# More output buffers, a moved half of one output stage, an earlier weight quarter, and zero matmuls in waits: attention and a swish layer on one core

## The chip, the core and the metric

The kernel runs on one core of a Trainium2 chip (trn2). The core has five engines with a queue of instructions each: TensorE (PE; its weight loads are PEld), VectorE (DVE), ScalarE (ACT), GpSimd (POOL) and SyncE (SP). GpSimd, SyncE and ScalarE also issue DMAs, which 16 DMA engines carry out. The metric is the device time of one execution in microseconds (us), less is better.

## What is computed

For each of 8 batches and 8 heads: attention over 576 positions with a window of 128, a bias that falls linearly with distance, and head dimension 64. The heads of a token side by side make 512 features, and the 4608 tokens then go through two matrix products with a swish between them.

```python
scores = q @ k.T / 8 - slope[h] * abs(rel)      # only 0 <= rel < 128
attn   = softmax(scores)
x      = (attn @ v) as [4608 tokens, 512]
h      = x @ w_in                                # 512 -> 2048
g      = h * sigmoid(beta * h)
out    = g @ w_out                               # 2048 -> 512
```

## The kernel before

A batch goes through these helpers. `load_pair` (L100), `load_tail`, `load_qk` and `load_v` each start a DMA on SP into a staging buffer (`fst`, 16 of them, L78) and a cast to bf16 on GpSimd. Batches 0 to 2 are transposed on TensorE (`TP`, `TT`: transposes into PSUM, then a VectorE copy), the later ones by transposing DMAs on SP (`TD`, L223). `SC` (L235) makes a block of scores (L240, L254) in a PSUM tile of the pool `psum_s`, which has one buffer, and ScalarE takes the exponentials (L262, L267). `PV` (L283) multiplies by the values for four heads (g = 0 or 1) of one block of 128 queries, into PSUM of `psum_t` (two buffers, shared with all transposes), and normalizes: a reciprocal and a multiply on VectorE, or, for batch 0 and g = 1, four multiplies on ScalarE (L305). `X` (L312) transposes the normalized block through `psum_t` into `XT`, with a ScalarE copy for batch 0 and a VectorE copy otherwise.

The layer works in nine groups of 512 tokens. `HS(g, j)` (L330) is one of 16 slices of the hidden layer: four matmuls of 512 columns (L337) into `psum_h`, a tanh on ScalarE (L342) and a combining instruction on VectorE (L343). Groups 0 to 2 let every second slice use `psum_o` as well, so four buffers instead of two (L334). `OS(g, i, n)` (L347) is a quarter of the output of 128 tokens, four matmuls (L353) into `psum_o`; after the fourth quarter ScalarE evicts the tile to an output buffer (`osb`, three of them, L84, L359) and GpSimd issues its store (L361).

The order of TensorE is the order of the program text; that of the other engines is planned by the compiler around it. TensorE does, in this order: batch 0's transposes, scores and values (L454 to L479); the 16 slices of group 0 with batch 1 spread between them (L494); the 16 slices of group 1 alone (L499); the 32 quarters of the outputs of groups 0 and 1 with batch 2 spread between them (L502); group 2's slices with batch 3 (L507, no output among them); then for each later group its slices in turn with the quarters of the group before, and the remaining batches between them; last the 16 quarters of group 8 (L517). `spread` sets so many attention steps behind each item that they end three items before the end of the list.

W1 is loaded in four quarters and W2 too, by DMAs on GpSimd that also cast (L172, L175). The first two quarters of W1 are issued behind the cast of the fourth block of V of batch 0 (L431), the third and fourth behind casts of batch 1 (L437), W2 behind those of V of batch 1.

Of the kernel before, what the change touches and what calls it, by code (L numbers as in the profile page):

```python
# [11 lines left out]
BF16 = mybir.dt.bfloat16  # L12
F32 = mybir.dt.float32
P = 128
# [3 lines left out]
def kernel(  # L18
# [10 lines left out]
    nc = tc.nc  # L29
# [38 lines left out]
    kpos = const.tile([P, 1], F32, name="kpos")  # L68
    bias = const.tile([P, 2, H], F32, name="bias")
    VS = [const.tile([P, NQB, H, D + 2], BF16, name=f"vs{i}") for i in range(2)]  # L70
    QK = [const.tile([P, 2, NP, NQB * P], BF16, name=f"qkT{i}") for i in range(2)]
# [5 lines left out]

    fst_pool = ctx.enter_context(tc.tile_pool(name="fst", bufs=16))  # L78
    bst_pool = ctx.enter_context(tc.tile_pool(name="bst", bufs=8))
# [3 lines left out]
    sig_pool = ctx.enter_context(tc.tile_pool(name="sig", bufs=3))  # L83
    osb_pool = ctx.enter_context(tc.tile_pool(name="osb", bufs=3))  # L84
    psum_s = ctx.enter_context(tc.tile_pool(name="psum_s", bufs=1, space=bass.MemoryType.PSUM))
# [13 lines left out]

    def load_pair(b, p):  # L100
        t = bst_pool.tile([P, 2, LA, 2, D], BF16, name="bst", tag="bst")
        for i, src in enumerate((q, k)):
            f = fst_pool.tile([P, 2, LA, D], F32, name="fst", tag="fst")
            nc.sync.dma_start(
                out=f[:].rearrange("r h a d -> r h (a d)"),
                in_=src[b, 2 * p : 2 * p + 2, 0:LM].rearrange("h (r a) d -> r h (a d)", a=LA),
            )
            c = nc.gpsimd.tensor_copy(out=t[:, i], in_=f[:].rearrange("r h a d -> r a h d"))
        staged[b, p] = t
        return c  # L110
# [14 lines left out]
    def load_v(b, sb):  # L125
# [10 lines left out]
        allow_small_or_imprecise_dtypes=True,  # L136
    )
    nc.vector.tensor_scalar(out=ident[:], in0=diff[:], scalar1=0.0, scalar2=None, op0=ALU.is_equal)
    nc.vector.memset(QK[0][:, :, :, S:], 0.0)
# [50 lines left out]
    def load_beta():  # L190
        bps = psum_t.tile([P, NFF], F32, name="bps", tag="t")
        nc.tensor.transpose(out=bps[:], in_=bflat[:], identity=ident_f[:])
        return nc.vector.tensor_scalar_mul(beta_h[:], bps[:], 0.5)


# [86 lines left out]

    def PV(b, qb, g):  # L283
        nq = ROWS[qb]
        vs = VS[b % 2]
        if g == 0:
            xns[b, qb] = xn_pool.tile([P, H, D], BF16, name="xn", tag="xn")
        xn = xns[b, qb]
        pv = psum_t.tile([P, 4, 66], F32, name="pv", tag="t")
        for hl in range(4):  # L290
            h = 4 * g + hl
            if qb:
                nc.tensor.matmul(  # L293
                    pv[:, hl, 0 : D + 1], lhsT=weights(b, qb - 1, h, 1),
                    rhs=vs[:, qb - 1, h, 0 : D + 1], start=True, stop=False,
                )
            nc.tensor.matmul(  # L297
                pv[:, hl, 0 : D + 1], lhsT=weights(b, qb, h, 0),
                rhs=vs[:, qb, h, 0 : D + 1], start=qb == 0, stop=True,
            )  # L300
        zs = xn_pool.tile([P, 4, 1], F32, name="zs", tag="zs")
        rcp = nc.vector.reciprocal(out=zs[0:nq], in_=pv[0:nq, :, D : D + 1])  # L302
        if b == 0 and g:
            for hl in range(4):
                nc.scalar.mul(xn[0:nq, 4 + hl, :], pv[0:nq, hl, 0:D], zs[0:nq, hl, :])  # L305
            return rcp
        nc.vector.tensor_tensor(  # L307
            out=xn[0:nq, 4 * g : 4 * g + 4, :], in0=pv[0:nq, :, 0:D],
            in1=zs[0:nq].broadcast_to([nq, 4, D]), op=ALU.mult,
        )  # L310

    def X(b, qb):  # L312
# [17 lines left out]
    def HS(g, j):  # L330
        if j == 0:
            gts[g] = gt_pool.tile([P, NFF, TOKG], BF16, name="gT", tag="gT")
        c0 = (g * TOKG) % XTR
        pool, tag = (psum_o, "ops") if g < 3 and j % 2 else (psum_h, "hps")  # L334
        hps = pool.tile([P, TOKG], F32, name="hps", tag=tag)
# [11 lines left out]
    def OS(g, i, n):  # L347
# [9 lines left out]
        if n == 3:  # L357
            osb = osb_pool.tile([P, DM], F32, name="osb", tag="osb")
            nc.scalar.mul(osb[:], ops_[:], 0.5)  # L359
            row0 = g * TOKG + i * P  # L360
            nc.gpsimd.dma_start(out=out[row0 : row0 + P, :], in_=osb[:])  # L361

# [63 lines left out]
    with tc.manual_schedule(engines={mybir.EngineType.PE}):  # L426
# [7 lines left out]
        for p in range(NP):  # L434
            c = load_pair(1, p)
            if p % 2:
# [10 lines left out]
        with tc.tile_pool(name="psum_x", bufs=2, space=bass.MemoryType.PSUM) as psum_x:  # L447
            pools = [psum_x, psum_x, psum_s]

            def sc0(m, p):  # L450
                SC(0, m, p, pools[0])
                pools.append(pools.pop(0))

            TP(0, 0)  # L454
            TP(0, 1)
# [17 lines left out]
        psum_o = ctx.enter_context(  # L473
            tc.tile_pool(name="psum_o", bufs=2, space=bass.MemoryType.PSUM))
        for qb in range(NQB):
            c = PV(0, qb, 1)
            if qb:
                X(0, qb - 1)
        X(0, NQB - 1)  # L479
        with tc.issue_after(c.ins):  # L480
# [20 lines left out]
        ahead(2, 1)()  # L501
        spread(os(0) + os(1), by_pair(2))  # L502
        todo = sum((by_block(b) for b in range(NTE, B)), [])
# [3 lines left out]
        for g in range(2, NTG):  # L507
            moe = hs(g)
            if g > 2:
                moe = sum(([a, c] for a, c in zip(moe, os(g - 1))), [])  # L510
# [38 lines left out]
```

## Time and profile before

| | us |
|---|---|
| median of 3 runs (lowest to highest) | 367.81 (366.11 to 368.38) |
| the profiled execution | 365.09 |
| its span, first to last instruction | 363.3 |
| TensorE busy | 327.8 (90%) |
| ScalarE, VectorE, GpSimd busy | 215.7, 203.0, 102.2 |
| HBM read, written | 36.71 MB, 9.44 MB |

The profile shows one execution. A line of the busy table gives an engine's busy time in a stretch; the slices cut the span into 40 parts of 9.08 us and give tenths. The granted clock is TensorE's, as a share of its full 2.4 GHz; the lower level is 0.50. A wait is put down to the instruction or DMA that released it last. Times within the span count from its first instruction.

### The profile page before, as it was taken

Reading aid. Unit: us, or ns where it says so; the run is one execution under the profiler, and the core shown is the slowest. Engines: PE = TensorE matmul, PEld = TensorE weight load, DVE = VectorE, ACT = ScalarE, POOL = GpSimd, SP = SyncE. Lnnn points to the kernel's source line nnn. Section 1 sums busy time; section 2 is a strip of 40 time slices with the busy share of each in tenths; the row PEclk is TensorE's granted clock in tenths of the full one; section 3 lists DMA queues with packets and bytes.
Section 4 is the critical chain, followed back from the end, with each engine's and each line's share of the span. In section 5 each row is a group of like instructions: output and inputs, shape, how many; then the busy total and the mean of one; then the engine's idle time right before and its main releaser. Section 6 shows DMA issues by size and latency. Waiting matters only on the chain.

```text
span 363.3 us, 6317 instructions
## 1 busy us (share of the span) xinstructions
PE 327.8 (90%) x2317; PEld 159.9 (44%) x2361; DVE 203.0 (56%) x441; ACT 215.7 (59%) x427; POOL 102.2 (28%) x176
## 2 busy tenths in 40 slices
PE   2967998999659797899999999999999999999993
PEld 1444454454325343444444445444444445444441
DVE  5435768766325288656566756675766556433300
ACT  4575784756241588575675876686768674444410
POOL 6672552424364063126145010200000000100111
PEclk9976999999969989999999999999999999999998
DMA  7999999979999698979899513200000000010021
GB/s 193 246 251 230 229 212 229 181 154 160 188 257 242 133 251 142 174 142 209 188 211 250 105 43 81 80 28 32 31 29 31 29 31 31 37 50 32 29 87 58
DMA packets 125886, 48.26 MB, mean 133 GB/s; under 512 B 113296, under 2 KB 123552, under 8 KB 125856
## 3 DMA queue, kind: packets, MB, share of 16 engines
q1 hardware_dynamic: 118720, 34.22, 50.4%
q0 software_dynamic: 7104, 13.63, 14.1%
q8 instruction: 18, 0.29, 0.3%
q14 instruction: 12, 0.10, 0.1%
q10 hardware_dynamic: 32, 0.01, 0.0%
HBM read 36.71 MB, written 9.44 MB: 127 GB/s over the span
## 4 chain that ended last, share of the span: by engine, by line
PE 42%; issue 34%; DMA 6%; DVE 5%; ACT 4%; POOL 3%; SPq 3%; POOLq 0%; ACTq 0%
PE hps L337 18%; PE ops L353 13%; PE sps L254 3%; DMA fst<-in_v_dram 3%; POOL out_dram L361 3%; PE sps L240 2%; PE pv L297 2%; PE pv L293 2%; SPq L94 2%; SPq L226 2%; PE xt L320 1%; DVE gT L343 1%; DMA fst<-in_q_dram 1%; ACT xn L305 1%; DVE xn L307 1%
## 5 line engine op out<-in xcount | busy, mean ns | idle before, releaser
L337 PE MATMUL hps<-XT,W 128*128 128x512 bf16 x550 | 143.8, 385 | 1.7 <-issue 0.9
L353 PE MATMUL ops<-W,gT 128*128 128x512 bf16 x559 | 143.9, 383 | 1.1 <-issue 0.3
L342 ACT ACTIVATE sig<-hps,beta_h 128x512 bf16<-128x512 f32 x144 | 99.5, 692 | 72.8 <-PE hps L337 63.4
L343 DVE SCALAR_TENSOR_TENSOR gT<-sig,hps 128x512 bf16<-128x512 bf16 x144 | 98.4, 684 | 56.3 <-ACT sig L342 55.7
L267 ACT ACTIVATE pt<-sps,bias 128x256 bf16<-128x256 f32 (+1 forms) x192 | 75.2, 478 | 11.1 <-PE sps L254 10.9
L337 PEld LDWEIGHTS <-W 128*128 128x128 bf16 x576 | 52.0, 99 | 57.6 <-issue 6.2
L353 PEld LDWEIGHTS <-gT 128*128 128x128 bf16 x576 | 51.6, 98 | 53.4 <-issue 3.2
L361 POOL DMA_DIRECT2D out_dram<-osb x36 | 19.5, 542 | 137.8 <-ACT osb L359 137.8
L121 POOL CAST bst<-fst 128x512 bf16<-128x512 f32 (+1 forms) x50 | 32.3, 649 | 65.3 <-DMA fst<-in_q_dram 46.1
L271 DVE TENSOR_TENSOR pt<-pt,mask 128x1024 bf16<-128x1024 bf16 x48 | 33.9, 705 | 22.9 <-ACT pt L267 22.6
L359 ACT ACTIVATE osb<-ops 128x512 f32<-128x512 f32 x36 | 21.6, 601 | 42.0 <-PE ops L353 34.1
L254 PE MATMUL sps<-qkT 64*128 64x256 bf16 (+2 forms) x320 | 25.9, 258 | 10.1 <-ACT pt L267 9.8
L126 POOL CAST vs<-fst 128x512 bf16<-128x512 f32 (+1 forms) x40 | 24.5, 619 | 35.2 <-DMA fst<-in_v_dram 18.5
L307 DVE TENSOR_TENSOR xn<-pv,zs 128x256 bf16<-128x256 f32 (+1 forms) x75 | 31.7, 422 | 2.4
L302 DVE RECIPROCAL zs<-pv 128x4 f32<-128x4 f32 (+1 forms) x80 | 14.1, 177 | 29.7 <-PE pv L297 29.3
L297 PE MATMUL pv<-vs,pt 128*128 128x65 bf16 x320 | 29.8, 197 | 0.7 <-DVE pt L271 0.4
L297 PEld LDWEIGHTS <-pt 128*128 128x128 bf16 x320 | 22.6, 99 | 13.4 <-issue 4.2
L293 PE MATMUL pv<-vs,pt 128*128 128x65 bf16 x256 | 24.7, 196 | 4.1 <-ACT xn L305 1.8
L254 PEld LDWEIGHTS <-qkT 64*128 64x128 bf16 x320 | 10.9, 95 | 37.5 <-issue 36.3
L293 PEld LDWEIGHTS <-pt 128*128 128x128 bf16 x256 | 20.3, 100 | 9.2 <-DVE xn L307 2.9
L262 ACT ACTIVATE pt<-sps 128x1024 bf16<-128x1024 f32 x16 | 16.0, 1027 | 11.8 <-PE sps L254 11.6
L325 DVE COPY XT<-xt 128x512 bf16<-128x512 bf16 (+1 forms) x36 | 13.9, 389 | 15.6 <-PE xt L320 15.1
(41 smaller groups left out, 125.6 us busy)
## 6 DMA issues: line engine op xcount, KB each, us to landing
out_dram<-osb POOLq DMA_DIRECT2D x36, 256.0 KB, 2.3
fst<-in_q_dram SPq DMA_DIRECT2D x32, 256.0 KB, 5.1
fst<-in_k_dram SPq DMA_DIRECT2D x32, 256.0 KB, 5.2
fst<-in_v_dram SPq DMA_DIRECT2D x32, 256.0 KB, 5.5
W<-in_moe_w_in_dram POOLq DMA_DIRECT2D x4, 512.0 KB, 11.7
W<-in_moe_w_out_dram POOLq DMA_DIRECT2D x4, 512.0 KB, 13.8
fst<-in_q_dram SPq DMA_DIRECT2D x8, 128.0 KB, 5.4
fst<-in_k_dram SPq DMA_DIRECT2D x8, 128.0 KB, 5.3
```

The costliest lines, as they stand in the source:

```text
L121: c = nc.gpsimd.tensor_copy(out=t[0 : ROWS[sb], i], in_=load_rows(src, b, sb))
L254: nc.tensor.matmul(o, lhsT=qk[64 * e : 64 * e + 64, 1, p, P * kb : P * kb + P], rhs=qk[64 * e : 64 * e + 64, 0, p, P * kb : P * kb + nq], ...
L267: nc.scalar.activation(out=pt[:, e, cols], in_=sps[:, e, cols], func=ACTF.Exp, scale=qscale, bias=bias[:, half, h : h + 1],)
L271: nc.vector.tensor_tensor(out=pt[:], in0=pt[:], in1=masks[m][:].rearrange("p (o c) -> p o c", o=1).broadcast_to([P, 2, 512]), op=ALU.mult,)
L293: nc.tensor.matmul(pv[:, hl, 0 : D + 1], lhsT=weights(b, qb - 1, h, 1), rhs=vs[:, qb - 1, h, 0 : D + 1], start=True, stop=False,)
L297: nc.tensor.matmul(pv[:, hl, 0 : D + 1], lhsT=weights(b, qb, h, 0), rhs=vs[:, qb, h, 0 : D + 1], start=qb == 0, stop=True,)
L307: nc.vector.tensor_tensor(out=xn[0:nq, 4 * g : 4 * g + 4, :], in0=pv[0:nq, :, 0:D], in1=zs[0:nq].broadcast_to([nq, 4, D]), op=ALU.mult,)
L337: nc.tensor.matmul(hps[:], lhsT=W1[:, c, bass.ts(j, P)], rhs=XT[:, c, c0 : c0 + TOKG], start=(c == 0), stop=(c == NDM - 1),)
L342: nc.scalar.activation(out=sig[:], in_=hps[:], func=ACTF.Tanh, scale=beta_h[:, j : j + 1])
L343: nc.vector.scalar_tensor_tensor(out=gts[g][:, j, :], in0=sig[:], scalar=1.0, in1=hps[:], op0=ALU.add, op1=ALU.mult)
L353: nc.tensor.matmul(ops_[:], lhsT=gT[:, j, i * P : i * P + P], rhs=W2[:, j, :], start=(j == 0), stop=(j == NFF - 1),)
L361: nc.gpsimd.dma_start(out=out[row0 : row0 + P, :], in_=osb[:])
```

## The change

The output buffers go from three to six and the staging buffers from 16 to 14. The stores of the last group are issued by SP. The last eight of the 16 output quarters of group 1 move from the stage of batch 2 into group 2's slices, one behind every two slices, and group 2's slices use `psum_h` alone. The first q load of batch 1 waits for a one-element GpSimd copy into its staging buffer that reads the first quarter of W1, so it comes after that quarter. In batch 0, for g = 1, the values go to `psum_h` and `psum_o` in turn and VectorE normalizes them in one multiply. `idle` issues matmuls of a zero tile with itself, whose result nobody reads: nine of 512 columns ahead of the first transposes, and, in batch 0's g = 1, one behind each of the five `PV` and of the first four `X`.

```diff
+    zero = const.tile([P, 512], BF16, name="zero")
...
-    fst_pool = ctx.enter_context(tc.tile_pool(name="fst", bufs=16))
+    fst_pool = ctx.enter_context(tc.tile_pool(name="fst", bufs=14))
...
-    osb_pool = ctx.enter_context(tc.tile_pool(name="osb", bufs=3))
+    osb_pool = ctx.enter_context(tc.tile_pool(name="osb", bufs=6))
...
-    def load_pair(b, p):
+    def load_pair(b, p, hold=None):
         t = bst_pool.tile([P, 2, LA, 2, D], BF16, name="bst", tag="bst")
         for i, src in enumerate((q, k)):
             f = fst_pool.tile([P, 2, LA, D], F32, name="fst", tag="fst")
+            if hold is not None:
+
+                nc.gpsimd.tensor_copy(out=f[0:1, 0, 0, 0:1], in_=hold)
+                hold = None
             nc.sync.dma_start(
...
+    nc.vector.memset(zero[:], 0.0)
...
+    def idle(to, n):
+
+        for _ in range(n):
+            nc.tensor.matmul(
+                to, lhsT=zero[:, 0:P], rhs=zero[:], start=True, stop=True, skip_group_check=True
+            )
...
-    def PV(b, qb, g):
+    def PV(b, qb, g, pool=None):
...
-        pv = psum_t.tile([P, 4, 66], F32, name="pv", tag="t")
+        pool, tag = pool or (psum_t, "t")
+        pv = pool.tile([P, 4, 66], F32, name="pv", tag=tag)
...
-        if b == 0 and g:
-            for hl in range(4):
-                nc.scalar.mul(xn[0:nq, 4 + hl, :], pv[0:nq, hl, 0:D], zs[0:nq, hl, :])
-            return rcp
         nc.vector.tensor_tensor(
             out=xn[0:nq, 4 * g : 4 * g + 4, :], in0=pv[0:nq, :, 0:D],
             in1=zs[0:nq].broadcast_to([nq, 4, D]), op=ALU.mult,
         )
+        return rcp
...
-        pool, tag = (psum_o, "ops") if g < 3 and j % 2 else (psum_h, "hps")
+        pool, tag = (psum_o, "ops") if g < 2 and j % 2 else (psum_h, "hps")
...
-            nc.gpsimd.dma_start(out=out[row0 : row0 + P, :], in_=osb[:])
+            (nc.sync if g == NTG - 1 else nc.gpsimd).dma_start(out=out[row0 : row0 + P, :], in_=osb[:])
...
-            c = load_pair(1, p)
+            c = load_pair(1, p, None if p else W1[0:1, 0, 0:1])
...
+            w = psum_t.tile([P, 512], F32, name="w", tag="t")
+            idle(w[:], 9)
             TP(0, 0)
             TP(0, 1)
...
+        w = psum_s.tile([P, 2, 512], F32, name="w", tag="sps")
         for qb in range(NQB):
-            c = PV(0, qb, 1)
+            c = PV(0, qb, 1, (psum_o, "ops") if qb % 2 else (psum_h, "hps"))
+            idle(w[:, 0, :], 1)
             if qb:
                 X(0, qb - 1)
+                idle(w[:, 1, :], 1)
         X(0, NQB - 1)
...
-        spread(os(0) + os(1), by_pair(2))
+        o1 = os(1)
+        spread(os(0) + o1[0:8], by_pair(2))
...
             moe = hs(g)
-            if g > 2:
+            if g == 2:
+                moe = sum((moe[2 * n : 2 * n + 2] + [o1[8 + n]] for n in range(8)), [])
+            else:
                 moe = sum(([a, c] for a, c in zip(moe, os(g - 1))), [])
```

## Rows read from the trace of the kernel before

**Rows 1.** The page's forty slices of 9.08 us, busy tenths: TensorE and DMA.

```profile
PE   2967998999659797899999999999999999999993
DMA  7999999979999698979899513200000000010021
```

**Rows 2.** Busy time by stage: stretch, length, engines with counts, clock, DMA share, GB/s.

```profile
21.80:30.20 8.40, 4.95 (x56) 4.03 (x57) 2.66 (x26) 6.42 (x24) 4.36 (x8) 0.59 1.18 238
30.20:33.50 3.30, 3.08 (x9) 1.13 (x8) 0.61 (x1) 1.06 (x2) 1.47 (x3) 0.50 1.21 204
74.80:96.90 22.10, 21.77 (x173) 10.64 (x174) 13.02 (x25) 11.65 (x29) 5.76 (x11) 1.00 0.92 156
96.90:104.10 7.20, 0.03 (x3) 0.05 (x4) 0.05 (x1) 2.06 (x5) 4.72 (x8) 0.84 1.29 242
104.10:109.00 4.90, 4.84 (x27) 2.30 (x28) 2.00 (x5) 1.84 (x5) 3.73 (x5) 0.54 1.26 257
121.10:150.50 29.40, 23.03 (x181) 10.96 (x184) 21.42 (x44) 22.93 (x49) 8.84 (x15) 0.94 1.01 187
150.50:344.20 193.70, 192.13 (x1288) 91.73 (x1313) 115.36 (x234) 125.83 (x249) 33.10 (x57) 1.00 0.39 82
```

**Rows 3.** Waits of ScalarE and TensorE, 74 to 121 us: total us, times, longest.

```profile
ACT osb L359 <- DMA out_dram<-osb: 7.9, 1, 7.9
PE sps L254 <- ACT pt L267: 7.2, 1, 7.2
```

**Rows 4.** Timeline of GpSimd, 45 to 135 us: the first store (start, us, instruction).

```profile
97.47 0.57 POOL L361 DMA_DIRECT2D out_dram<-osb  x1
```

**Rows 5.** Matmuls early (timeline) and later (chain), and the page's group of exponentials.

```profile
9.08 1.06 PE L240 MATMUL sps<-table,sident 128*128 128x512 bf16 x2
...
112.09 0.86 PE ops L353 x4
...
L267 ACT ACTIVATE pt<-sps,bias 128x256 bf16<-128x256 f32 (+1 forms) x192 | 75.2, 478 | 11.1 <-PE sps L254 10.9
```

**Rows 6.** Timelines of ScalarE and TensorE, 22 to 31 us, idle time before in brackets.

```profile
25.11 0.93 ACT L305 ACTIVATE xn<-pv,zs 128x64 bf16<-128x64 f32 x4 [0.43 <-DVE zs L302]
...
30.20 0.58 PE L337 MATMUL hps<-XT,W 128*128 128x512 bf16 x1
```

**Rows 7.** GpSimd's timeline; W1's first quarter to landing (KB, us); all quarters.

```profile
18.14 1.67 POOL L173 DMA_DIRECT2D W<-in_moe_w_in_dram  x2
19.79 0.64 POOL L126 CAST vs<-fst 64x512 bf16<-64x512 f32 x1
...
W<-in_moe_w_in_dram POOLq DMA_DIRECT2D x1, 512.0 KB, 10.8
...
DMA to landing us min/median/max: 8.5/11.7/13.8
```

**Rows 8.** Timelines: first load and last V cast of batch 1, and its use.

```profile
14.49 0.62 SPq L104 DMA_DIRECT2D fst<-in_q_dram  x1
...
45.78 0.65 POOL L126 CAST vs<-fst 64x512 bf16<-64x512 f32 x1
...
52.42 0.20 PE L293 MATMUL pv<-vs,pt 128*128 128x65 bf16 x1
```

**Rows 9.** Timelines: batch 4's last transposing DMA, and its first scores.

```profile
120.83 1.20 SPq L226 DMA_TRANSPOSE qkT<-bst  x1
...
151.47 0.39 PE L254 MATMUL sps<-qkT 64*128 64x256 bf16 x4
```

**Rows 10.** Stores and SP's first load to landing; drains (min/median/max ns, first and last start).

```profile
out_dram<-osb POOLq DMA_DIRECT2D x36, 256.0 KB, 2.3
...
fst<-in_q_dram SPq DMA_DIRECT2D x1, 256.0 KB, 3.3
...
L544 POOLq DRAIN  x3: 51/102/4223, 358.1 to 362.8; - x3
L544 SPq DRAIN  x3: 7/7/13, 360.8 to 362.6; - x3
```

## The prediction

> **What bounds the kernel now.** I read the page's forty slices first, then busy time by stage, then what TensorE waits for in the poor stages, then the queues that end those waits.
>
> The slices [rows 1] show two halves. From 154 us on TensorE is busy nine tenths or more of every slice until the last; before that there are dents from 18 to 36 us, from 91 to 109 and from 118 to 154. DMA is busy six tenths or more, mostly nine, up to 200 us: whatever is moved there meets a nearly full resource. The stages [rows 2] put numbers on it. From 150.5 to 344.2 us TensorE is busy 192.13 of 193.70 us, so an edit can only save time before that or behind the last matmul.
>
> Four places are loose. (1) 21.8 to 33.5 us: TensorE is busy 4.95 of 8.40 us, then 3.3 us of hidden-layer matmuls run at clock 0.50, the lower of the two levels (1.2 GHz). (2) 96.9 to 104.1 us: 0.03 us of TensorE work in 7.20, and the next 4.9 us at a mean clock of 0.54. (3) 121.1 to 150.5 us: TensorE 23.03 of 29.40, ScalarE 22.93, VectorE 21.42. (4) The tail, in which nothing computes.
>
> **The change part by part.**
>
> *Six output buffers (place 2).* TensorE waits 7.2 us for an exponential, and ScalarE waits 7.9 us to evict an output tile, because the buffer's store has not landed [rows 3]. The exponential stands behind that eviction on ScalarE. The first store was issued only at 97.47 us [rows 4], among GpSimd's casts of later loads. With three buffers the fourth tile needs it to have landed; with six the seventh does. In the new order six tiles are evicted in this stage (four of group 0, two of group 1), and the seventh comes in the middle of the next, over 10 us after that landing. So the 7.2 us go. With them goes the lower clock behind the hole: 4.9 us at mean 0.54 is (1 - 0.54)/0.5 = 92% at half rate, 4.5 us, of which half, 2.2 us, comes back. Sum 9.4 us. What is late next: up to the hole TensorE was busy 21.77 of 22.10 us [rows 2], so no data of batch 2 is near.
>
> *Half of O of group 1 inside H of group 2 (places 2 and 3).* Eight items of four matmuls leave the stage that ends at 121.1. An item takes 0.86 us at full clock [rows 5], so 6.9 us leave a stage that TensorE bounds. The attention work is covered more thinly there: all score blocks share one PSUM buffer, and the exponentials of one block take 75.2 us / 48 = 1.57 us [rows 5], with scores and two handoffs some 2.2 us, about what TensorE will have between two of them. I give back 1 us for that. In the next stage TensorE has 23.03 us, of which (1 - 0.94)/0.5 x 29.4 / 2 = 1.8 us is half-clock excess, so 21.3 us at full clock; with 6.9 added, 28.2. ScalarE has 22.93 and two evictions more, VectorE 21.42. Bounds: 28.2 us if all of it falls into holes, 29.4 + 6.9 = 36.3 if none does. The lower is nearer, since the holes (6.4 us) are there because too little TensorE work lies between the pieces of attention; but the hidden layer of group 2 loses the two PSUM buffers that it borrowed, so I leave 3 us of stalls: 31.2 us. Net: 6.9 - 1 - (31.2 - 29.4) = 4.1 us, between -1 and 7.1.
>
> *Batch 0's second four heads (place 1).* Five steps (values, normalizing, transposes, copy) take the 8.4 us from 21.8 to 30.2, with TensorE waiting in each for ScalarE's four multiplies, 0.93 us [rows 6]. After, one VectorE multiply does it and the values lie in PSUM buffers of their own, so TensorE can run ahead of the normalizing. Its own work in a step is 8 x 65 columns of values, 4 x 128 of transposes and 2 x 512 of zeros, 2056 columns: by the 0.86 us of 4 x 512 that is 0.86 us at full rate, 1.72 at half; I take 1.25, since small matmuls hardly reach the rate by columns. Five steps less a transpose, 0.7 + 4 x 1.25, and 0.4 us for the last one: from a start at 21.0 us the first hidden-layer matmul is at 27.1, and it is at 30.20 now: 3.1 us. (The start is 0.8 us earlier than now because these values no longer queue for the two shared buffers, and the last V cast of batch 0 ends at 20.4 [rows 7].) If the clock holds, the 3.3 us at half rate behind it cost half, 1.6 us less. If it doesn't, the steps take as long as now: gain 0.
>
> *Nine zero matmuls ahead.* Two matmuls of 512 columns take 1.06 us at 9.08 [rows 5], against 0.86 for four later: TensorE starts at half rate. Nine take 9 x 0.43 = 3.9 us, from about 1.3 us on, so they may delay the first transposes by 0.5 us, hidden since the next ones wait for a load. If full rate lasts to the scores, up to 2 us of work is saved there; but five exponentials in a row and the last V cast stand behind it, so 0 to 1 us, and it is in the start at 21.0.
>
> *W1's first quarter ahead of batch 1.* It is issued at 18.14 us and lands 10.8 us later, at 28.9 [rows 7]: too late for 27.1. The new one-element copy on GpSimd reads that quarter, and the first q load of batch 1 waits for the copy. Behind that load in SP's queue stand the other 14 loads of the batch (from 14.49 us on now [rows 8]); behind the copy on GpSimd, all their casts and W1's third and fourth quarters. Alone, the quarter takes between 3.4 us (a store of 256 KB takes 2.3 alone [rows 10]; twice the bytes at 238 GB/s [rows 2] is 1.1 more) and 8.5, the shortest of W1 in traffic [rows 7]. I take 5, near the low end because little else moves: about 17.6 + 5 = 22.6 us. The Trainium skill, "DMA: Bandwidth & Descriptors", section "Anatomy of one DMA — SWDGE (gpsimd) path", gives 2.0 us and 436 GB/s for such a DMA, an estimate of 4.4 us for the 1 MB read; by that it lands at 22.0, and no run here shows it yet.
>
> The price: batch 1 starts 8 us later. Meanwhile the DMA engines do W1's first half (from 18 to 45 us they did four quarters and 4.2 MB; at 238 GB/s that leaves 2.3 us a quarter), so 2 to 3 us of a full resource are lost. The last V cast of batch 1 now ends at 46.4 us and TensorE wants it at 52.4 [rows 8]: 6 us of slack, against TensorE 4.7 earlier and data 3 later. I take 1.5 us of waits (0 to 7). Place 1 in all: 3.1 + 1.6 - 1.5 = 3.2 us, between -3 and 6.
>
> *14 staging buffers.* Two loads fewer run ahead, 2 to 3 us. Batch 4's last transposing DMA is issued at 120.8 us and its first scores run at 151.5 [rows 9]: of these 30 us the earlier TensorE takes 17. Nothing.
>
> *Last stores by SyncE (place 4).* The last store is issued at 358.1 and takes 2.3 us to land, 360.4; SP's drain stands at 360.8, but GpSimd's lasts 4.2 us from 358.1 to 362.3 [rows 10], and the end, 363.3, is 1 us behind it. With SP the landing takes between 2.3 (alike) and 3.3 us (SP's first load), and GpSimd's drain has nothing left to wait for: the end is some 1 us behind SP's drain, 361.5 to 362.5. I take 1.4 us; below, 0. The Trainium skill, the same page, section "Latency and other measured facts", puts the first byte at 1 us for GpSimd's DMAs and 0.6 for the others. By that difference alone the gain would be an estimate of 0.4 us; the drain's row speaks for more.
>
> **Sum.** 9.4 + 4.1 + 3.2 + 1.4 = 18.1 us from the profiled execution's 365.09, so 347.0 there. That execution lies 2.7 us under the median of the runs, 367.81; against that, 349.7. I say 350.
>
> **Rivals.** (A) *Batch 1 comes late.* The quarter takes 8.5 us or more and the casts and W1's last quarter stall the stage by 7 us: place 1 gives -3, total 12, 356. For it: DMA share of 1.2 in these stages [rows 2]. Against: the slack at each use. (B) *The O half is only moved.* Two PSUM buffers for H and one for scores make group 2's stage wait for ScalarE and VectorE: 36.3 us, that part gives -1, time 355. For it: these two have 22.9 and 21.4 of 29.4 us. (C) *The clock stays low in place 1* in spite of the zero matmuls: place 1 gives -1.5 instead of 3.2, 354.5. (D) *Slower.* Everything of batch 1 hangs on one landing. At 13.8 us, the longest of W1 in traffic [rows 7], batch 1 starts at 31.4, its last V is near 58 (46.4 + 16.9 - 4.6) where 47.7 is wanted, and place 1 loses 11. It decides from a landing at 36 us, where it eats the 14.9 us of the other parts; at 40 it would be 372. (E) *The stores are not the cause*: another wait fills the hole at 96.9, total about 9, 359.
>
> **Chances.** Forecast 0.56, A 0.15, B 0.11, C 0.09, D 0.03, E 0.06. The forecast's own range is 345 to 354; with A, B and C 344 to 358, which leaves out D, E and some of A. About 1% is what a measurement of this kernel can tell from no change. Faster by over 1%: all but D and a little of E, 0.94; same 0.03; slower 0.03.
>
> **What would show it.** No eviction waiting for a store; no hole over 2 us and clock 1.00 between 75 and 110 us; the first hidden-layer matmul at about 27 us at full rate; W1's first quarter landed at about 23; under 2 us of TensorE waits for batch 1's data; group 2's stage 29 to 33 us long; the end 1.4 us nearer to the last eviction. The forecast is wrong if the hole comes back elsewhere before 150 us, or if the stages behind, now full, begin to wait for loads.

## The result, and the profile after

The changed kernel takes 346.09 us (median of four runs, 345.59 to 346.28); the kernel before, beside it, 367.24 us. The ratio is 0.942, with an interval of 0.939 to 0.946. The profiled execution of after takes 346.27 us, its span is 344.5 us.

In the page's slices of after (8.61 us each; TensorE, its granted clock, DMA) the dents of [rows 1] are gone. From the 7th slice to the last but one TensorE is busy nine tenths or more, but for one slice of eight tenths, and the clock stands at full speed everywhere:

```profile
PE   7988979999998999999999999999999999999995
PEclk9999999999999999999999999999999999999999
DMA  6999999999999999959999796100000000010021
```

Busy time of after by stage, with the columns of [rows 2]: the last steps of batch 0, group 0's slices with batch 1, the outputs with batch 2, group 2's slices with batch 3, and the stages behind:

```profile
20.00:24.80 4.80, 4.55 (x67) 3.02 (x64) 3.79 (x19) 2.35 (x5) 0.73 (x2) 1.00 1.24 208
24.80:57.10 32.30, 28.11 (x252) 14.18 (x252) 22.94 (x61) 19.17 (x25) 16.81 (x27) 1.00 1.13 238
70.95:103.04 32.09, 30.33 (x269) 15.91 (x268) 19.87 (x44) 15.93 (x39) 11.97 (x20) 1.00 1.02 176
103.04:134.20 31.16, 28.51 (x218) 13.37 (x217) 22.18 (x45) 23.88 (x51) 12.26 (x20) 1.00 1.12 207
134.20:326.00 191.80, 191.80 (x1306) 90.87 (x1305) 114.86 (x232) 124.51 (x246) 38.90 (x66) 1.00 0.49 100
```

I set the starts of the stages side by side, since a difference between two executions then shows in the stage where it arises. HS(g) is the first hidden-layer matmul of group g, all times in us from the first instruction:

| | before | after | gain |
|---|---|---|---|
| HS(0) starts | 30.20 | 24.80 | 5.4 |
| from there to HS(1): batch 1's stage | 30.85 | 32.34 | -1.5 |
| HS(1) to the first output matmul | 13.81 | 13.81 | 0 |
| from there to HS(2): batch 2's stage | 46.22 | 32.09 | 14.1 |
| HS(2) to group 2's first output: batch 3's stage | 29.4 | 31.1 | -1.7 |
| from there to the end of the last hidden-layer matmul | 192.0 | 192.0 | 0 |
| last eviction to the end of the span | 5.47 | 3.06 | 2.4 |

Before rounding the gains add up to 18.8 us, which is 363.3 - 344.5. The same 192.0 us in both kernels show that the full stages were not touched.

ScalarE's waits in after between 70 and 133 us (total us, times, longest) answer [rows 3]. Not one is for a store:

```profile
ACT osb L370 <- PE ops L364: 9.8, 4, 4.0
ACT pt L280 <- PE sps L267: 6.9, 7, 3.6
ACT sig L353 <- PE hps L348: 6.7, 11, 2.4
```

### The profile page after: what moved, and what is told of

It reads as the page before. It is cut to its first block, busy times and chain, and to the rows that moved or that the text cites. A ratio compares the mean times of both kernels' runs of the same rounds, so it can differ in the third digit from the quotient of the medians.

```text
span 344.5 us, 6371 instructions
## 1 busy us (share of the span) xinstructions
PE 327.8 (95%) x2379; PEld 157.4 (46%) x2379; DVE 206.2 (60%) x447; ACT 211.5 (61%) x407; POOL 100.6 (29%) x173
## 4 chain that ended last, share of the span: by engine, by line
PE 71%; DMA 15%; SPq 5%; ACT 3%; DVE 3%; issue 1%; POOL 1%; POOLq 0%
PE ops L364 34%; PE hps L348 28%; DMA fst<-in_v_dram 7%; DMA fst<-in_k_dram 5%; PE sps L267 4%; SPq L95 3%; ACT pt L280 2%; SPq L109 2%; PE xt L331 2%; PE pv L311 2%; DMA W<-in_moe_w_in_dram 2%; DMA fst<-in_q_dram 2%; PE pv L307 1%; DVE pt L284 1%; DVE gT L354 1%
## 5 line engine op out<-in xcount | busy, mean ns | idle before, releaser
L348 PEld LDWEIGHTS <-W 128*128 128x128 bf16 x576 | 51.3, 97 | 57.1 <-issue 4.8
L372 POOL DMA_DIRECT2D out_dram<-osb x32 | 17.4, 543 | 107.4 <-ACT osb L370 107.4
L284 DVE TENSOR_TENSOR pt<-pt,mask 128x1024 bf16<-128x1024 bf16 x48 | 35.2, 733 | 17.5 <-ACT pt L280 17.0
L317 DVE TENSOR_TENSOR xn<-pv,zs 128x256 bf16<-128x256 f32 (+1 forms) x80 | 33.6, 422 | 2.4
L311 PE MATMUL pv<-vs,pt 128*128 128x65 bf16 x320 | 28.2, 193 | 2.3 <-POOL vs L131 2.3
L267 PE MATMUL sps<-qkT 64*128 64x256 bf16 (+2 forms) x320 | 25.2, 252 | 2.9 <-ACT pt L280 2.9
L316 DVE RECIPROCAL zs<-pv 128x4 f32<-128x4 f32 (+1 forms) x80 | 14.1, 178 | 22.6 <-PE pv L311 21.9
L311 PEld LDWEIGHTS <-pt 128*128 128x128 bf16 x320 | 21.8, 97 | 9.9 <-issue 0.8
L307 PE MATMUL pv<-vs,pt 128*128 128x65 bf16 x256 | 24.4, 193 | 1.5 <-DVE xn L317 0.8
L307 PEld LDWEIGHTS <-pt 128*128 128x128 bf16 x256 | 19.9, 98 | 10.2 <-issue 3.2
```

The costliest lines, as they stand in the source:

```text
L267: nc.tensor.matmul(o, lhsT=qk[64 * e : 64 * e + 64, 1, p, P * kb : P * kb + P], rhs=qk[64 * e : 64 * e + 64, 0, p, P * kb : P * kb + nq], ...
L284: nc.vector.tensor_tensor(out=pt[:], in0=pt[:], in1=masks[m][:].rearrange("p (o c) -> p o c", o=1).broadcast_to([P, 2, 512]), op=ALU.mult,)
L307: nc.tensor.matmul(pv[:, hl, 0 : D + 1], lhsT=weights(b, qb - 1, h, 1), rhs=vs[:, qb - 1, h, 0 : D + 1], start=True, stop=False,)
L311: nc.tensor.matmul(pv[:, hl, 0 : D + 1], lhsT=weights(b, qb, h, 0), rhs=vs[:, qb, h, 0 : D + 1], start=qb == 0, stop=True,)
L317: nc.vector.tensor_tensor(out=xn[0:nq, 4 * g : 4 * g + 4, :], in0=pv[0:nq, :, 0:D], in1=zs[0:nq].broadcast_to([nq, 4, D]), op=ALU.mult,)
L348: nc.tensor.matmul(hps[:], lhsT=W1[:, c, bass.ts(j, P)], rhs=XT[:, c, c0 : c0 + TOKG], start=(c == 0), stop=(c == NDM - 1),)
```

## The experiments

The changed kernel was run ahead of these and not beside them. The kernel before ran beside each group of them, with medians of 366.12, 365.17 and 366.67 us of seven runs each. So I take no difference to after's 346.09 under about 1.5 us for a fact unless a row shows where it lies. Each number below is a median of four runs unless said otherwise.

### Six buffers alone, and three in the changed kernel

`osb6` is the kernel before with the two pools resized:

```diff
-    fst_pool = ctx.enter_context(tc.tile_pool(name="fst", bufs=16))
+    fst_pool = ctx.enter_context(tc.tile_pool(name="fst", bufs=14))
-    osb_pool = ctx.enter_context(tc.tile_pool(name="osb", bufs=3))
+    osb_pool = ctx.enter_context(tc.tile_pool(name="osb", bufs=6))
```

> The kernel before with six output buffers and 14 staging buffers, nothing else changed. All eight tiles of groups 0 and 1 are still evicted in one stage. If the buffers are what the hole hung on: the hole of 7.2 us at 97 us and the 2.2 us of half clock behind it go, and at most a small wait is left at the seventh tile; 8 to 10 us less than before, 357 to 360. Rival, that the hole comes back at the next late thing (casts, the one score buffer): 361 to 366.

Measured: 356.81 us, 9.3 less than before; the ratio is 0.975 (0.971 to 0.980). Busy time of batch 2's stage and of group 2's slices in it, columns as above:

```profile
75.30:112.10 36.80, 36.73 (x301) 18.71 (x300) 20.14 (x44) 16.96 (x40) 16.71 (x27) 1.00 0.98 189
112.10:142.00 29.90, 23.41 (x186) 10.93 (x185) 21.04 (x44) 22.93 (x49) 9.56 (x17) 0.94 0.92 190
```

The stage goes from 46.22 to 36.86 us, 9.36 less, and TensorE has no idle time left in it. The hole, the low clock behind it and the missing output buffer are one thing. The two staging buffers fewer cost nothing that shows.

`osb3` is the changed kernel with three output buffers again:

```diff
-    osb_pool = ctx.enter_context(tc.tile_pool(name="osb", bufs=6))
+    osb_pool = ctx.enter_context(tc.tile_pool(name="osb", bufs=3))
```

> The changed kernel (346.1 us) with three output buffers again, all else kept. If the late stores are the cause of the hole: the fourth tile of the stage of batch 2 is ready at about 92 us and must wait for a store that is issued at 91 and lands at 94 to 96, the fifth and sixth for stores issued at 100 and later; ScalarE waits for stores 5 to 12 us in sum, the stage grows from 32.1 us by as much, time 350 to 358. Rival, that another part of the change took the hole away: no wait for a store, 345 to 347.

Measured: 352.63 us, 6.5 more than after. The wait is there, but not where I had put it. Busy time of `osb3` in batch 2's stage and behind it:

```profile
70.30:102.40 32.10, 30.35 (x270) 15.90 (x268) 19.28 (x44) 15.32 (x38) 11.71 (x19) 1.00 0.93 166
102.40:140.70 38.30, 29.74 (x217) 13.58 (x216) 22.25 (x45) 24.21 (x52) 15.55 (x25) 0.91 0.99 199
```

Its ScalarE waits between 70 and 135 us, and its TensorE waits between 70 and 140:

```profile
ACT osb L370 <- DMA out_dram<-osb: 16.7, 3, 10.5
```

```profile
PE sps L267 <- ACT pt L280: 7.5, 4, 6.2
```

Batch 2's stage is as long as in after (32.08 against 32.09 us). The longest wait ends at 105.42 us, so the hole falls at the start of group 2's slices, and from the start of these slices to the end of the last hidden-layer matmul it takes 230.31 us against 223.09. ScalarE waits 16.7 us for stores; TensorE loses 7.2 by it, in the hole and at the lower clock behind it.

### All of group 1's outputs in batch 2's stage

```diff
-        pool, tag = (psum_o, "ops") if g < 2 and j % 2 else (psum_h, "hps")
+        pool, tag = (psum_o, "ops") if g < 3 and j % 2 else (psum_h, "hps")
...
-        spread(os(0) + o1[0:8], by_pair(2))
+        spread(os(0) + o1, by_pair(2))
...
-            if g == 2:
-                moe = sum((moe[2 * n : 2 * n + 2] + [o1[8 + n]] for n in range(8)), [])
-            else:
+            if g > 2:
```

> The changed kernel with all 32 output quarters of groups 0 and 1 in the stage of batch 2 and four PSUM buffers for group 2's slices, all else kept. If the moved half fills holes: the stage of batch 2 grows from 32.1 to 38 us (6.9 of moved work less 1 of waits for the one score buffer), group 2's stage shrinks from 31.1 to 27 to 29, sum +2 to +5, time 348 to 351. Rival, that the half is only moved from one full stage to another: both stages change by 6.9 us, time 345.5 to 347.

Measured: 349.73 us, 3.6 more than after. Its two stages, the second from the first hidden-layer matmul of group 2 to group 2's first output, and what TensorE waits for in the second:

```profile
70.20:107.00 36.80, 36.73 (x301) 18.73 (x300) 19.90 (x44) 16.96 (x41) 14.32 (x23) 1.00 0.89 183
107.04:136.00 28.96, 22.14 (x186) 10.77 (x185) 20.81 (x44) 22.77 (x49) 11.21 (x19) 1.00 1.03 200
```

```profile
PE sps L267 <- ACT pt L280: 3.5, 4, 1.9
PE xt L331 <- DVE xn L317: 2.2, 2, 1.3
```

The time is as expected, and so is group 2's stage: I had expected 27 to 29 us without the moved work, and it takes 28.96, at full clock, with TensorE busy 22.14 us only. TensorE waits there for exponentials and for normalized blocks. In after it is busy 28.48 us of 31.13. So of some 6.9 us of moved work about 4.7 fall into these holes, and 2.2 make the stage longer. In batch 2's stage the move takes away 4.77 us (36.86 - 32.09), where I had expected 5.9, and leaves TensorE idle 1.8 us where it was idle 0.1. Together that is 4.77 - 2.17 = 2.6 us.

The two profiled executions differ by 3.4 us, not by 2.6. `omove` begins group 1's slices 0.8 us earlier (56.37), but from group 2's first output to the end of the last hidden-layer matmul it takes 193.6 us, where before and after take 192.0. In that part the waits of TensorE show one, of 1.48 us, for a normalized block. The block comes late because VectorE, ahead of it, takes 3.56 us for a multiply by the mask whose median is 0.69, beside four casts on GpSimd (timelines of VectorE, GpSimd and TensorE):

```profile
196.40 3.56 DVE L284 TENSOR_TENSOR pt<-pt,mask 128x1024 bf16<-128x1024 bf16 x1 [0.23 <-ACT pt L280]
196.85 2.27 POOL L131 CAST vs<-fst 128x512 bf16<-128x512 f32 x4
200.56 0.29 PE L331 MATMUL xt<-ident,xn 128*128 128x128 bf16 x2 [1.48 <-DVE xn L317]
```

What stretched the multiply was not tested, nor whether the executions without a profile have it too. So 2.6 us are shown for the moved half, and the rest of the 3.6 is open.

### The last stores by GpSimd again

```diff
-            (nc.sync if g == NTG - 1 else nc.gpsimd).dma_start(out=out[row0 : row0 + P, :], in_=osb[:])
+            nc.gpsimd.dma_start(out=out[row0 : row0 + P, :], in_=osb[:])
```

> The changed kernel with the last four stores on GpSimd again. From the last eviction's end to the end of the span it is 5.5 us before and 3.1 after. If the queue of the last stores makes the whole of that: 5.5 us again, time +2.4, 348 to 349. Rival, that the stores gain only what a DMA from GpSimd takes longer to its first byte (an estimate of 0.4 us from the Trainium skill, DMA: Bandwidth & Descriptors, Latency and other measured facts): 346.3 to 347.

Measured: 347.57 us, 1.5 more. The end of the span is 5.28 us behind the last eviction, against 3.06 in after. Drains of `pstore`, then those of after, then after's last stores (ns min/median/max, first and last start):

```profile
L563 POOLq DRAIN  x3: 51/93/4223, 340.8 to 345.5; - x3
L563 SPq DRAIN  x3: 7/7/13, 343.5 to 345.3; - x3
```

```profile
L563 POOLq DRAIN  x3: 51/102/3991, 327.9 to 344.2; - x3
L563 SPq DRAIN  x3: 7/7/13, 343.6 to 343.9; - x3
```

```profile
L372 SPq DMA_DIRECT2D out_dram<-osb x4: 332/344/373, 331.1 to 341.5; - x4
```

In `pstore` GpSimd's drain starts at the last store, at 340.8 us, and takes 4.2, as in [rows 10]; in after it begins behind GpSimd's own last store at 327.9 us and is hidden. Time to landing, of the last two stores of after, then of the last of `pstore` (KB, us):

```profile
out_dram<-osb SPq DMA_DIRECT2D x2, 256.0 KB, 2.0
```

```profile
out_dram<-osb POOLq DMA_DIRECT2D x1, 256.0 KB, 2.3
```

The landing itself differs by 0.3 us and the issue by 0.2 (0.34 against 0.54); the rest of the 2.2 us is the drain. In the spans the difference is 1.3 us and not 2.2, because the last eviction came 0.9 us earlier in this execution, ahead of which the edit changes nothing but three stores.

### The old normalizing

The four ScalarE multiplies and the shared PSUM buffers come back, and the zero matmuls stay:

```diff
+        if b == 0 and g:
+            for hl in range(4):
+                nc.scalar.mul(xn[0:nq, 4 + hl, :], pv[0:nq, hl, 0:D], zs[0:nq, hl, :])
+            return rcp
...
-            c = PV(0, qb, 1, (psum_o, "ops") if qb % 2 else (psum_h, "hps"))
+            c = PV(0, qb, 1)
```

> The changed kernel with the normalizing of batch 0's second four heads as before: four ScalarE multiplies, values in the two PSUM buffers shared with the transposes; zero matmuls kept. Theory: a step takes 1.6 to 1.85 us again instead of 0.9, the first hidden-layer matmul comes 3 to 4.5 us later, the waits for batch 1 (3.2 us) go: +1 to +2.5, 347 to 348.5. Rival, that the steps were slow by the clock alone: step 1.0 us, 345.7 to 346.5.

Measured: 349.45 us, 3.4 more, about twice what I expected. Its last steps of batch 0 and its stage of batch 1:

```profile
20.50:30.40 9.90, 6.44 (x95) 4.11 (x96) 4.35 (x31) 7.52 (x27) 3.11 (x6) 1.00 1.14 237
30.40:60.00 29.60, 27.35 (x249) 14.32 (x253) 21.84 (x49) 19.18 (x25) 16.17 (x27) 1.00 1.21 236
```

The first hidden-layer matmul is at 30.43 us, as before (30.20), but at full clock. A step takes 1.63 us (26.72 to 28.35) instead of 0.89 in after. Batch 1 is now never late, so the stage is short (29.54 us), and group 1's slices start at 59.97 us instead of 57.14: 2.8 of the 3.4 us. The other 0.6 lies behind group 2's first output, where this execution too has a long multiply by the mask (2.46 us at 197.48) and a wait of TensorE behind it (0.39 us). The run brings back the ScalarE multiplies and the shared buffers together, so it does not tell which of the two makes the step long.

### The hold of batch 1 taken away, and put elsewhere

`nohold`:

```diff
-            c = load_pair(1, p, None if p else W1[0:1, 0, 0:1])
+            c = load_pair(1, p)
```

> The changed kernel without the copy that holds batch 1's first q load. Theory: W1's first quarter shares the DMA engines again and lands at 27 to 29 us instead of 22.7, so the first hidden-layer matmul comes at about 28 instead of 24.8; in return batch 1 is early and the 3.2 us of waits for its casts and V go. Sum 0 to +2: 346 to 348. Rival, that the hold is worth its whole 3 to 4 us (the waits come from W1's later quarters, not from the hold): 349 to 351. Rival, that it only costs (a DMA pause of 3 us): 343 to 345.5.

Measured: 345.3 us (344.36 to 346.99), no difference to after that can be told. W1's first quarter, issued at 18.17 us, now takes 8.8 to land, until 27.0:

```profile
W<-in_moe_w_in_dram POOLq DMA_DIRECT2D x1, 512.0 KB, 8.8
```

The first hidden-layer matmul waits for it, 0.7 us, and comes at 27.01. The stage behind, however, has no wait for batch 1's casts and is as short as in `oldpv`:

```profile
27.00:56.60 29.60, 27.36 (x249) 14.35 (x254) 21.94 (x51) 18.83 (x24) 14.86 (x24) 1.00 1.08 224
```

In after the slices start 2.2 us earlier, and this is what TensorE waits for between 24.8 and 58 us:

```profile
PE pv L311 <- POOL vs L131: 1.7, 2, 1.4
PE tps L216 <- POOL bst L113: 1.5, 2, 1.3
```

3.2 us of waits for batch 1's casts. Group 1's slices start at 56.57 us without the hold and at 57.14 with it. What the hold gives at the front, batch 1 takes back.

`hold1` holds the second pair of batch 1 instead of the first, so fewer loads stand behind the hold. `hold1q` also spaces W1's quarters out, one behind each pair of batch 1:

```diff
-            c = load_pair(1, p, None if p else W1[0:1, 0, 0:1])
+            c = load_pair(1, p, W1[0:1, 0, 0:1] if p == 1 else None)
```

```diff
                     load_w1(0)
-                    load_w1(1)
...
-            if p % 2:
+            if p:
                 with tc.issue_after(c.ins):
-                    load_w1(2 + p // 2)
+                    load_w1(p)
```

> The changed kernel with the held load one pair later, so that both loads of the first pair of batch 1 and one of the second go ahead of W1's first quarter, in the 3 us in which the DMA engines stand still while GpSimd prepares it. If those 3 us are lost time: the quarter lands as early as now (22 to 23.5 us), the waits for batch 1's casts and V shrink from 3.2 to 1 us or less, 343.5 to 345. Rival, that the early loads delay the quarter as much as they help: 345.5 to 347.

> As the one before, and W1's second quarter is issued behind the casts of the second pair of batch 1 instead of right behind the first quarter. If the second quarter delays batch 1 by its 2.2 us of DMA time: the waits for batch 1 go altogether, 343 to 344.5. Rival, that the later quarters then come late for slices 4, 8 and 12 of group 0: 346 to 349.

Measured: `hold1` 345.85 us (345.04 to 348.67), the same as after, where I had hoped for a gain; the quarter lands at 23.5, the slices start at 25.62 us, the stage takes 30.77, and group 1's slices start at 56.39. `hold1q` 347.54 us (347.19 to 349.38), about 1.5 slower, in the rival's range but not for its reason: no slice waits for a quarter of W1. Its profiled execution is its slowest, and there TensorE (26 to 61 us) waits for the cast of the batch's tail, which itself sat 3.24 us waiting for its load:

```profile
PE tps L229 <- POOL tail L119: 2.6, 1, 2.6
```

### The zero matmuls

`nozero` leaves out all of them, `nonine` the nine ahead, `onlynine` those in the steps:

```diff
-            w = psum_t.tile([P, 512], F32, name="w", tag="t")
-            idle(w[:], 9)
```

```diff
-        w = psum_s.tile([P, 2, 512], F32, name="w", tag="sps")
...
-            idle(w[:, 0, :], 1)
...
-                idle(w[:, 1, :], 1)
```

> The changed kernel without any zero matmul. Theory: the clock is at the lower level up to about 13 us and again behind the values of batch 0, as before; the steps of the second four heads take longer and the first hidden-layer matmuls run at half rate, first hidden-layer matmul at 26 to 28 us instead of 24.8, 1 to 1.6 us lost behind it, of which the waits for batch 1 give some back: +1 to +4, 347 to 350. Rival, that the other PSUM buffers and the VectorE multiply keep TensorE busy enough without them: 345.5 to 346.5.

> The changed kernel without the nine zero matmuls ahead, those in the steps of the second four heads kept. Theory: half rate up to about 13 us, the last exponentials of batch 0 some 2 us later (they end at 17.8 us now), full rate from there on; W1's first quarter at 22.7 is no longer waited for. First hidden-layer matmul 1 to 2.5 us later, half of it swallowed by the waits for batch 1: 346.5 to 348. Rival, that the load of V sets the start and the nine are worth nothing: 345.7 to 346.5.

> The changed kernel with the nine zero matmuls ahead, without those in the steps of the second four heads. Theory: TensorE is left with 0.9 us of work in steps that wait for VectorE and ScalarE, the clock falls near 22 to 25 us and the first hidden-layer matmuls run at half rate: +1 to +3, 347 to 349. Rival, that the steps are dense enough without them: 345 to 346.3, each zero matmul of 0.2 us being saved.

Measured: `nonine` 346.24 us (345.1 to 346.62) and `onlynine` 345.95 us (345.76 to 347.26), both the same as after. `nozero` 347.48 us, but from 345.57 to 348.46, so 0 to 1.4 us that these runs don't settle. Its profiled execution is its slowest, and its span is 2.2 us longer than after's. All of that arises before group 1's slices, which start at 59.31 us instead of 57.14. W1's first quarter is issued at 18.68 us and ends the hold only at 25.73; the loads of batch 1 start behind it, and TensorE waits 2.7 us for their casts although its first slice starts as late as 27.11 us. GpSimd's timeline and TensorE's waits from there to 61 us:

```profile
25.73 0.18 POOL L107 CAST fst<-W 1x1 f32<-1x1 bf16 x1 [4.75 <-DMA W<-in_moe_w_in_dram]
```

```profile
PE pv L311 <- POOL vs L131: 1.4, 2, 0.9
PE tps L216 <- POOL bst L113: 1.3, 1, 1.3
```

I had expected `onlynine` to lose 1 to 3 us to the lower clock. It doesn't: even `nozero` runs the steps at full clock, with TensorE busy 3.63 of 5.10 us:

```profile
22.00:27.10 5.10, 3.63 (x72) 2.72 (x71) 4.78 (x18) 2.27 (x4) 0.73 (x2) 1.00 1.06 174
```

In before it was 4.95 of 8.40 us at 0.59 [rows 2]. So full clock comes with the zeros and the old long steps (`oldpv`) and with the short steps and no zeros (`nozero`); with both, one is spare. The old steps without the zeros, but with the hold, were not run.

### The kernel before, profiled once more

No edit: `before2` is to show where two executions of it differ.

> The kernel before, unchanged, for a second profile: its runs without a profile lie up to 3 us above the profiled 365.09. If the length of the hole at 97 us varies from run to run: the hole and the waits for the store differ from 7.2 us while every stage behind 150 us takes 191.8 us again. Rival, that all stages stretch alike: hole 7.2 us, the difference spread.

Measured: 366.61 us in one run, span 364.8. Its hole, the time behind it and the stage of group 2's slices, to be held against [rows 2]:

```profile
97.00:104.00 7.00, 0.84 (x7) 0.43 (x7) 0.69 (x1) 2.25 (x6) 4.27 (x8) 0.88 1.30 251
104.00:110.00 6.00, 5.78 (x34) 2.77 (x34) 1.99 (x7) 1.97 (x5) 4.73 (x9) 0.57 1.29 243
120.90:152.00 31.10, 24.09 (x181) 11.33 (x184) 21.77 (x44) 23.00 (x49) 10.44 (x17) 0.89 1.03 196
```

Group 2's slices take 31.1 us at clock 0.89 here, 29.4 at 0.94 in the first profile. These 1.7 us are the whole difference of the two spans (1.5). Batch 2's stage, with the hole, takes 46.0 us against 46.2, so the hole is not what differs, as I had thought it might; nor do all stages stretch alike: the full stages behind agree (192.0 us both).

## Why the prediction was right, and where its steps were off

The prediction said 350.0 us, its forecast's own range was 345 to 354, and 346.09 came. Rivals B, C and E fell: group 2's stage is 31.13 us and not 36.3, the clock is 1.00 in place 1, and no wait replaced the stores. Of A and D, batch 1 coming late, a part is true: 3.2 us of waits, where I had allowed for 1.5 and A had 7.

**Six output buffers: right.** 9.4 us predicted, 9.36 less in the stage of `osb6`. It was right because the hole and the low clock behind it were read as one item from [rows 2 to 4]. The size depends on the order around it: in the changed order three buffers cost 7.2 us, and in another stage.

**Half of O of group 1: group 2's stage right, batch 2's cover mis-sized.** Predicted 4.1 us. Beyond what the buffers alone give, before and after differ by 4.77 - 1.70 = 3.1 us in the two stages; `omove` against after gives 2.6 by these stages and 3.6 by the medians. The stage of group 2 came out as I had built it: 28.2 us of TensorE work and 3 of stalls were predicted, 28.48 of work and 2.65 of idle time were measured. The thinner cover costs batch 2's stage 2.1 us (6.9 - 4.77), not 1; that is the term that I sized too small. I had also counted 1.8 us of half-clock work in before's stage as time to be had. `omove`, at full clock and with the same program order, is shorter by only 0.5 us (28.96 against 29.43), as TensorE's waits for exponentials and normalized blocks stay.

**Place 1: 3.2 us predicted, 3.9 measured, and a different carrier.** The first hidden-layer matmul is at 24.80 us, not 27.1. I took a step as 1.25 us, between the full rate by columns (0.86) and the half rate; it is 0.89, the full rate, and the steps begin at 20.0 us, not 21.0. Against that stand 3.2 us of waits for batch 1 instead of 1.5. The full clock behind the steps, which I had put at 1.6 us, shows in `oldpv`: with the first hidden-layer matmul at the same time as in before, its stage of batch 1 takes 29.54 us instead of 30.85, 1.3 less.

What I had not seen is that the early start and the waits hang together. With the first hidden-layer matmul anywhere from 24.55 to 27.01 us (after, `osb3`, `omove`, `pstore`, `nohold`, `hold1`, `nonine`, `onlynine`), group 1's slices start between 56.37 and 57.14 us. Where batch 1 is in time, the stage takes 29.6 us (`osb3` from 26.88 us, `nohold` from 27.01); where the slices start earlier, they wait for batch 1. `nozero` and `hold1q` start in that range too, or 0.1 us behind it, but group 1 starts at 59.31 and 60.65, since there batch 1's casts come later still. So the end of this stage hangs on the arrival of batch 1. After, `osb3`, `omove` and `pstore` do not differ up to there by any edit, and still their starts lie between 24.55 and 26.88 us: the 5.4 us of the table are one execution's, and the gain at group 1's start, 3.9 to 4.7 us in these four, is the steadier number. In these runs a start before about 27 us is worth nothing measurable, and the hold, the nine zeros and the zeros in the steps are each worth nothing measurable alone.

`oldpv` shows what carries most of place 1: without the one VectorE multiply and the PSUM buffers of their own the kernel loses 3.4 us, 2.8 of it before group 1's slices.

**W1's first quarter.** Issued at 17.32 us and landed at 22.8 (5.5 us), where I had 22.6. The Trainium skill's estimate ("DMA: Bandwidth & Descriptors", "Anatomy of one DMA — SWDGE (gpsimd) path") was 22.0 for an issue at 17.6; this trace has a landing of 5.5 us where it gives 4.4, so the measurement decides. My sentence that the quarter would be "too late for 27.1" without the hold is wrong: in `nohold` it lands at 27.0 and the matmul comes at 27.01.

GpSimd's timeline of after shows the hold at work, and SyncE's shows what it stops (start, us, instruction, idle time before):

```profile
17.32 1.68 POOL L179 DMA_DIRECT2D W<-in_moe_w_in_dram  x2
18.98 0.64 POOL L131 CAST vs<-fst 64x512 bf16<-64x512 f32 x1
22.96 0.18 POOL L107 CAST fst<-W 1x1 f32<-1x1 bf16 x1 [3.35 <-DMA W<-in_moe_w_in_dram]
```

```profile
13.90 0.57 SPq L109 DMA_DIRECT2D fst<-in_k_dram  x1
23.17 0.88 SPq L109 DMA_DIRECT2D fst<-in_q_dram  x2
```

One detail of the step was wrong: the pair's k load was planned ahead of the held q load, so 14 loads were held and not 15. SyncE then issues nothing from 14.5 to 23.17 us.

**Last stores by SyncE: 1.4 us predicted, 2.4 measured.** The reading of the drains [rows 10] was right. I took the landing by SP as 2.3 to 3.3 us; it is 2.0. The difference of first bytes in the Trainium skill (same page, "Latency and other measured facts") would have made an estimate of 0.4 us. `pstore` puts it at 2.2, so that difference isn't what sets this tail; GpSimd's drain is.

**From the profile to the median: the largest error.** The terms sum to 18.1 us, and 18.8 came between the two profiled executions. That they agree so well is in part luck: the moved half brought 1.0 less than its term, place 1 brought 0.7 more and the stores 1.0 more. The sum made 347.0 of the profiled 365.09, and 346.27 came. Then I added 2.7 us, since that execution of before lay under the median of its runs, and this took 347.0 to 349.7. That supposes that what makes before's runs differ stays in the kernel. `before2` shows where at least two executions differ: in group 2's slices at a varying clock, a stage that the change rebuilds. The four runs of after lie within 0.7 us; those of before range from 363.8 to 368.9. Four runs are few, though: those of `hold1` range from 345.04 to 348.67.

Still open: how much of `nozero`'s 0 to 1.4 us is real, and the long multiply by the mask in `omove`. No variant measurably beats the changed kernel. One without both the hold and the zeros was not run.

## What to carry to other kernels

When an engine waits for another engine, follow on to what that one was waiting for. Here a matmul waited for an exponential, the exponential stood behind an eviction, and the eviction waited for a store that had been issued late among casts; three buffers more bought 9.3 of the 21 us. Before starting a stage earlier, ask what its end is pinned to: with the next batch's data late, 2 us of earlier start were given back as waits, and three of the edits were worth nothing measurable. Work moved into a stage with holes is neither free nor full price: here 6.9 us of matmuls made group 2's stage 2.2 us longer, and the stage that they left lost 4.8 and not 6.9. To see this, cut a stage at the same instruction in every kernel compared.

## What the runs showed of the hardware

**GpSimd's DMAs started late into idle engines.** Between after's issue of two quarters of W1 at 17.32 us and their data there are some 2 us in which nearly nothing moves (busy time of after, the last two columns the DMA share and GB/s):

```profile
17.00:18.50 1.50, 1.01 (x28) 0.78 (x24) 0.96 (x5) 1.40 (x2) 1.50 (x3) 1.00 0.14 34
18.50:20.00 1.50, 0.78 (x20) 0.57 (x18) 0.90 (x3) 0.00 (x0) 1.12 (x2) 1.00 0.48 38
20.00:21.50 1.50, 1.31 (x22) 0.78 (x19) 1.36 (x6) 0.03 (x1) 0.00 (x0) 1.00 1.25 208
```

By the 208 GB/s that follow, 3 us are an estimate of 0.6 MB that is not moved there.

**The full clock of a short burst did not always last.** After and all its variants but `nonine` and `nozero` begin with the same nine zero matmuls from 1.2 us on, for 3.4 to 4.0 us. Between 9 and 13 us the granted clock was then 1.00 in after and `omove`, 0.60 in `pstore`, 0.58 in `hold1` and 0.50 in `onlynine`. Here is that stretch in after, then in `onlynine`:

```profile
9.00:13.00 4.00, 3.41 (x38) 1.79 (x36) 2.24 (x4) 2.52 (x3) 2.97 (x5) 1.00 1.24 280
```

```profile
9.00:13.00 4.00, 4.00 (x24) 1.71 (x23) 1.15 (x3) 1.20 (x2) 3.16 (x6) 0.50 1.17 277
```

The clock column can't be trusted so early: `osb3` shows 1.00 there, as before does, which has no zero matmuls. Two matmuls of 512 columns tell more. They take 0.59 us in after, but 1.06 in `osb3`, as in before [rows 5] and in `onlynine` (TensorE's timeline of after, then of `osb3`):

```profile
9.81 0.59 PE L253 MATMUL sps<-table,sident 128*128 128x512 bf16 x2
```

```profile
9.26 1.06 PE L253 MATMUL sps<-table,sident 128*128 128x512 bf16 x2
```

Where the clock lasted, the first hidden-layer matmul came at 24.80 and 24.55 us (after, `omove`); in `pstore`, `hold1`, `onlynine` and `osb3` it came at 25.60 to 26.88. Group 1's slices started at 56.4 to 57.1 us in all six. Why the clock lasts in one execution and not in the next isn't shown.

**A drain on GpSimd's queue** takes 4.0 to 4.2 us from its last store on, in before [rows 10], after and `pstore`, though the store lands in 2.3 us.
